# The output product of a fused attention and feed-forward kernel: from one product of 12 blocks to seven products of half blocks

## The chip, the cores and the metric

One core of one Trainium2 chip. The metric is device time in microseconds (us) of one execution of the whole program: the median of 3 runs is 566.71 us (566.59 to 567.5). Everything is computed on that core: TensorE (PE in the profile, with its weight loads PEld), VectorE (DVE), ScalarE (ACT), GpSimd (POOL) and SyncE (SP, here a queue that issues DMAs).

## The reference

A low-rank attention (keys and values are first projected from 1024 positions to 64) is followed by a gated feed-forward block. The output product, the last line, is what the change touches.

```python
# q, k, v: (8 batches, 8 heads, 1024, 64); E, F: (64, 1024)
k_proj = einsum('ks,bhsd->bhkd', E, k)
v_proj = einsum('ks,bhsd->bhkd', F, v)
attn   = softmax(q @ k_proj.T / sqrt(64))
x      = (attn @ v_proj), heads side by side     # 8192 x 512
g      = x @ w_gate                              # 512 -> 1536
h      = g * sigmoid(g) * (x @ w_val)            # 8192 x 1536
out    = h @ w_out                               # 1536 -> 512, float32
```

## The kernel before

**Chunks and steps.** The 8192 rows of `x` are worked through in 16 chunks `c` of 512 rows (two per batch `b`, c = 2b and 2b+1). A chunk has 12 steps `f`, one for each block of 128 of the 1536 inner columns. A step computes, transposed (128 inner columns on the partitions, 512 rows along the free side), the gate `f_g` and the value `f_v`: four matmuls of 128x128 by 512 columns each (`f_mm`, L440). ACT takes tanh of the gate's half (L452); DVE makes `s1 = (th + 1) * g` (L459) and `hT = s1 * v` in bf16 (L464). With the missing factor 0.5 that is `h`, and `hT[c]` is a tile of 128 x 12 x 512.

**The output product** of chunk c is spread over the steps of chunk c+1: `f_y(c, n)`, n = 0 to 11, one per step, four matmuls of 512 columns (L478). Three `f_y` make one block of 128 rows of the output: 12 matmuls accumulate over the 12 blocks of `hT`, ACT evicts them with scale 0.5 (L488), and SP sends 256 KB out (L490). The product of chunk 0 falls into steps 4 to 11 of chunk 1. The product of the last chunk is at the end, alone: 9 `f_y`, then `f_y_last`, whose last group is 12 matmuls of 192 columns.

**Attention runs ahead, in slots.** Each step t has two slots, 2t (between `f_g` and `f_v`) and 2t+1 (after `f_y`). `place(b)` (L508) puts the pieces of batch b into slots from s0 = 48(b-1) on, that is from the first step of chunk 2(b-1). For b = 3 and up: the projection `u_KV` in slot s0, `u_KT` in s0+3, eight score pieces `u_S` in slots s0+6, s0+9, ... s0+27, each followed one slot later by `u_R` (row sums and reciprocal on DVE, L346 and L348) and `u_N` (the normalising product on POOL, L361, 128x512), and eight `u_PV` (one matmul of 512 columns and an ACT copy). So the even chunk has six `u_N`, the last of them in the slot of step 11, and the odd chunk has two, after step 0 and in step 2. Batch 1 is placed by its own table: its score pieces lie in steps 5 to 10 of chunk 1, the transposing DMA `u_AD(1, 0)` (SP, L316) of the first four normalised pieces follows them, and `u_PV(1, 0, 0)` needs its result in step 10 of chunk 1.

**Loads are issued by POOL.** The K, V and two Q loads of batch b lie in four slots from 48(b-1)-24 on (for b = 3 from -20): in steps 0, 1, 2 and 3 of an odd chunk, and ahead of everything else of their slot. The loads of batches 4 to 7 are in chunks 5, 7, 9 and 11. At the start, POOL issues the loads of the weights, `wo` (the output weights, `load_wo`, L125) last, in two halves of six blocks.

**Buffers.** PSUM has eight banks: two for the gate, two for the value, one for the output product, three (`"a"`) for attention. `hT` has two buffers, `ysb` (the evicted output) three, K and V two each.

Every engine takes its instructions in the order in which the program issues them, so a line of Python that comes earlier is ahead in each engine's queue:

```python
for t in range(NIT):                       # L689
    c, f = divmod(t, NFT)
    f_g(c, f, i)
    run_slot(2 * t)
    f_v(c, f, i)
    for a in ypart.pop(t, ()):             # the f_y of chunk c-1
        f_y(*a)
    run_slot(2 * t + 1)
```

Of the kernel before, what the change touches and what calls it, by code (L numbers as in the profile page):

```python
# [28 lines left out]
CW = 512  # L29
NIT = B * CH * NFT  # L30
BY_DMA = [(b, ch) for b in range(1, B) for ch in range(CH)]


@with_exitstack
def kernel(
# [23 lines left out]
    w_pool = ctx.enter_context(tc.tile_pool(name="weights", bufs=1))  # L59
    kv_pool = ctx.enter_context(tc.tile_pool(name="kv", bufs=2))  # L60
    q_pool = ctx.enter_context(tc.tile_pool(name="qbf", bufs=4))
    aw = ctx.enter_context(tc.tile_pool(name="aw", bufs=2))
    x_pool = ctx.enter_context(tc.tile_pool(name="xT", bufs=2))
    h_pool = ctx.enter_context(tc.tile_pool(name="hT", bufs=2))
    fw = ctx.enter_context(tc.tile_pool(name="fw", bufs=3))
    y_pool = ctx.enter_context(tc.tile_pool(name="ysb", bufs=3))
    ps_g = ctx.enter_context(tc.tile_pool(name="psg", bufs=2, space=bass.MemoryType.PSUM))
    ps_v = ctx.enter_context(tc.tile_pool(name="psv", bufs=2, space=bass.MemoryType.PSUM))
    ps_y = ctx.enter_context(tc.tile_pool(name="psy", bufs=1, space=bass.MemoryType.PSUM))
    ps_a = ctx.enter_context(tc.tile_pool(name="psa", bufs=3, space=bass.MemoryType.PSUM))  # L70

# [10 lines left out]
    wv = w_pool.tile([P, NKT, DFF], BF16, name="wv")  # L82
    wo = w_pool.tile([P, NFT, DM], BF16, name="wo")

    kb, vb, qb, xT, hT = {}, {}, {}, {}, {}
# [45 lines left out]
    kvp = {}  # L131
    banks = {"a": (ps_a, "pa"), "g": (ps_g, "gps"), "v": (ps_v, "vps"), "y": (ps_y, "yps")}

    def bank(where, shape, dt, name):
        pool, tag = banks[where]
        return pool.tile(shape, dt, name=name, tag=tag)
# [152 lines left out]
    qT, ee, rr, AA, AT = {}, {}, {}, {}, {}  # L289

    def u_T(b, u, at="a", eng=nc.scalar):
        ch, w = divmod(u, 4)
        g, i = divmod(w, 2)
        ps = bank(at, [P, 4, P], BF16, "qTp")
        src = qb[b, ch]
        for n in range(4):
            nc.tensor.transpose(  # L297
                out=ps[:, n, :],
                in_=src[:, 4 * g + n, 2 * i : 2 * i + 2, :].rearrange("p j d -> p (j d)"),
                identity=ident_bf[:],  # L300
            )
        t = aw.tile([P, 4, P], BF16, name="qT", tag="qT", bufs=4)
        copy(eng, t[:], ps[:])
        qT[b, u] = t
# [46 lines left out]
    def u_N(b, u, eng=nc.gpsimd):  # L351
        ch, w = divmod(u, 4)
        g, i = divmod(w, 2)
        if (b, ch) in BY_DMA:
            if (b, ch, "d") not in AA:
                AA[b, ch, "d"] = aw.tile([P, 4, H, KP], BF16, name="AAd", tag="AAd")
            a = AA[b, ch, "d"][:, 2 * i : 2 * i + 2, 4 * g : 4 * g + 4, :]
        else:
            a = AA[b, u] = aw.tile([P, 2, 4, KP], BF16, name="AA", tag="AA", bufs=4)
            a = a[:]  # L360
        eng.tensor_tensor(  # L361
            out=a.rearrange("p j h k -> p h j k"),
            in0=ee.pop((b, u))[:],
            in1=rr.pop((b, u))[:].unsqueeze(3).to_broadcast([P, 4, 2, KP]),
            op=ALU.mult,
        )

    def u_A(b, u, eng=nc.vector):
        ch, w = divmod(u, 4)
        g, i = divmod(w, 2)  # L370
        if (b, ch) not in AT:
            AT[b, ch] = aw.tile([P, 4, NPAIR, P], BF16, name="AT", tag="AT")
        ps = ps_a.tile([P, 2, 2, P], BF16, name="aTp", tag="pa")
        a = AA.pop((b, u))
# [9 lines left out]
    def u_PV(b, ch, pr, eng=nc.scalar):  # L384
        if (b, ch) not in xT:
            xT[b, ch] = x_pool.tile([P, NPAIR, CW], BF16, name="xT", tag=f"xT{ch}")
        ps = ps_a.tile([P, CW], FP32, name="pv", tag="pa")
        nc.tensor.matmul(  # L388
            out=ps[:].rearrange("p (j t) -> p j t", t=P),
            lhsT=BDV[b % 2][:, pr, :],  # L390
            rhs=AT[b, ch][:, :, pr, :],
            start=True,
            stop=True,
        )
        copy(eng, xT[b, ch][:, pr, :], ps[:])

    def u_PV2(b, ch, g, i, eng):

        if (b, ch) not in xT:
            xT[b, ch] = x_pool.tile([P, NPAIR, CW], BF16, name="xT", tag=f"xT{ch}")  # L400
        ps = ps_a.tile([P, 2, CW // 2], FP32, name="pv", tag="pa")
        for n in range(2):
# [9 lines left out]
    def u_PV1(b, ch, pr, i, eng):  # L412

        ps = ps_a.tile([P, CW // 2], FP32, name="pv", tag="pa")
        nc.tensor.matmul(
# [39 lines left out]
    def f_v(c, f, i=None):  # L455
# [6 lines left out]
        if f == 0:  # L462
            hT[c] = h_pool.tile([P, NFT, CW], BF16, name="hT", tag="hT")
        nc.vector.tensor_tensor(out=hT[c][:, f, :], in0=s1[:], in1=ps[:], op=ALU.mult)  # L464

    yy = {}

    def f_y(c, n):
        i, part = divmod(n, 3)
        if part == 0:  # L470
            yy[c] = bank("gvgv"[i] if c == B * CH - 1 else "y", [P, DM], FP32, "yps")
        y_mm(c, i, range(4 * part, 4 * part + 4), slice(0, DM))
        if part == 2:
            y_out(c, i, slice(0, DM), nc.sync)

    def y_mm(c, i, fs, cs):
        for f in fs:
            nc.tensor.matmul(  # L478
                out=yy[c][:, cs],
                lhsT=hT[c][:, f, i * P : (i + 1) * P],  # L480
                rhs=wo[:, f, cs],
                start=(f == 0),
                stop=(f == NFT - 1),
            )

    def y_out(c, i, cs, eng):
        ysb = y_pool.tile([P, DM], FP32, name="ysb", tag="ysb")
        nc.scalar.activation(out=ysb[:, cs], in_=yy[c][:, cs], func=AF.Copy, scale=0.5)  # L488
        b, ch = divmod(c, CH)
        eng.dma_start(  # L490
            out=out[b * S : (b + 1) * S, :].rearrange("(p j) c -> p j c", j=NJ)[:, 4 * ch + i, cs],
            in_=ysb[:, cs],
        )

    def f_y_last(c, i):

        for cs, where in ((slice(0, 320), "v"), (slice(320, DM), "g")):
            yy[c] = bank(where, [P, DM], FP32, "yps")
            y_mm(c, i, range(NFT), cs)
            y_out(c, i, cs, nc.scalar)  # L500

# [39 lines left out]
    with tc.manual_schedule():  # L541
# [3 lines left out]
        for i in range(2):  # L545
# [3 lines left out]
            )  # L549
        ef = [const.tile([KP, S], dt, name=f"{n}raw") for n, dt in (("E", FP32), ("F", BF16))]  # L550
        nc.sync.dma_start(out=ef[0][:], in_=E)
# [130 lines left out]

        ypart = defaultdict(list)
        for c in range(B * CH - 1):
            for n in range(NFT):
                f = n if c else 4 + (2 * n + 1) // 3
                ypart[(c + 1) * NFT + f].append((c, n))

        for t in range(NIT):  # L689
            c, f = divmod(t, NFT)  # L690
            i = 1 if t < 2 else None
            f_g(c, f, i)
            run_slot(2 * t)
            f_v(c, f, i)
            for a in ypart.pop(t, ()):
                f_y(*a)
            run_slot(2 * t + 1)
        for n in range(9):
            f_y(B * CH - 1, n)
        f_y_last(B * CH - 1, 3)  # L700
        assert not slots and not ypart

# [28 lines left out]
```

## Time and profile before

| | |
|---|---|
| median of 3 runs | 566.71 us (566.59, 566.71, 567.5) |
| span of the profiled execution | 564.7 us |
| PE busy | 555.2 us, 98% of the span, 2917 matmuls in the trace |
| DVE, ACT, POOL busy | 339.5 (60%), 235.5 (42%), 111.9 us (20%) |
| matmuls of the output product (L478), 512 columns | 741 in the trace, 189.8 us |
| DVE `s1` and `hT` (128x512) | 679 and 688 ns each, 192 of each |
| ACT eviction of the output (128x512) | 597 ns each |
| POOL `u_N` (128x512) | 1041 ns each |
| last matmul group to the end of the span | eviction from 561.77 us, end at 564.7 |

The execution that was profiled has no run time of its own beside its span; the runs' median lies 2.0 us above the span, which is taken as a constant outside it. Times below are in us from the span's start. In the tables of the trace a line reads: start, duration, engine, source line, operation, output <- inputs, shape, count, and in brackets the idle time of that engine just before and what ended it. The duration of one matmul runs to the end of its result (379 ns for 512 columns) and overlaps the next one; the pace is read from the distance of starts. A few per cent of the matmuls are missing from the trace.

### The profile page before, as it was taken

The page shows a single profiled execution, that of the slowest core. Times are in us where ns is not written, and L with a number is a line of the kernel's source. Part 1 is how long each engine was busy: PE and PEld are TensorE (multiplying, and loading weights), DVE is VectorE, ACT ScalarE, POOL GpSimd, SP SyncE. Part 2 cuts the span into 40 slices and gives each one's busy share as a digit, 9 for nine tenths or more (in the row PEclk, how much of TensorE's full clock was granted, in tenths as well). Part 3 has the DMA queues.
Part 4 walks back from the last instruction along what each step waited for, and adds up shares of the span by engine and source line. Part 5 has one row for each costly group of instructions (what it writes and reads, how often), then busy time and mean ns, then how long its engine had stood idle before and what let it go on. Part 6 is the DMA issues. An engine that isn't in the chain of part 4 may idle for free.

```text
span 564.7 us, 7892 instructions
## 1 busy us (share of the span) xinstructions
PE 555.2 (98%) x2917; PEld 266.0 (47%) x2972; DVE 339.5 (60%) x579; ACT 235.5 (42%) x417; POOL 111.9 (20%) x126
## 2 busy tenths in 40 slices
PE   8999999999999999999999999999999999999997
PEld 4654544444444444444444444444444444444444
DVE  3787764766476655666556755667547665545550
ACT  3564352443444333543435434354243543443222
POOL 6851250133012400133002230024100220000000
PEclk9999999999999999999999999999999999999999
DMA  9999999529903894129920499106990212100012
GB/s 203 191 199 189 179 156 203 110 59 206 202 21 73 133 209 88 38 57 182 193 56 36 80 190 197 39 19 114 194 177 19 64 39 67 38 37 37 21 39 93
DMA packets 112215, 62.78 MB, mean 111 GB/s; under 512 B 66352, under 2 KB 103472, under 8 KB 112176
## 3 DMA queue, kind: packets, MB, share of 16 engines
q0 software_dynamic: 43952, 29.49, 36.5%
q1 hardware_dynamic: 67392, 31.46, 26.0%
q10 hardware_dynamic: 832, 1.31, 0.8%
q8 instruction: 23, 0.38, 0.3%
q14 instruction: 16, 0.13, 0.1%
HBM read 60.29 MB, written 16.78 MB: 136 GB/s over the span
## 4 chain that ended last, share of the span: by engine, by line
PE 95%; DMA 2%; POOL 1%; issue 1%; ACT 0%; POOLq 0%
PE vps L440 29%; PE yps L478 29%; PE gps L440 29%; PE sc L331 2%; PE pv L388 2%; DMA wv<-in_moe_w_val_dram 2%; PE kvp L151 2%; POOL vb L100 0%; POOL qb L109 0%; PE kvp L175 0%; PE kvp L190 0%; PE qTp L297 0%; PE kTp L252 0%; PE yps L440 0%; POOL kb L90 0%
## 5 line engine op out<-in xcount | busy, mean ns | idle before, releaser
L459 DVE SCALAR_TENSOR_TENSOR s<-th,gps 128x512 f32<-128x512 f32 x191 | 129.7, 679 | 132.7 <-ACT th L452 132.3
L440 PE MATMUL vps<-xT,wv 128*128 128x512 bf16 (+1 forms) x759 | 195.8, 377 | 1.9 <-DMA wv<-in_moe_w_val_dram 0.8
L440 PE MATMUL gps<-xT,wg 128*128 128x512 bf16 (+1 forms) x750 | 193.7, 377 | 0.8
L478 PE MATMUL yps<-wo,hT 128*128 128x512 bf16 (+2 forms) x765 | 192.6, 376 | 0.7
L452 ACT ACTIVATE th<-gps 128x512 f32<-128x512 f32 x191 | 114.0, 597 | 159.8 <-PE gps L440 139.9
L464 DVE TENSOR_TENSOR hT<-s,vps 128x512 bf16<-128x512 f32 x192 | 132.0, 688 | 20.8 <-DVE s L459 0.5
L361 POOL TENSOR_TENSOR AAd<-ee,rr 128x512 bf16<-128x512 f32 x56 | 58.2, 1041 | 340.9 <-issue 221.7
L478 PEld LDWEIGHTS <-hT 128*128 128x128 bf16 x780 | 76.2, 98 | 89.9
L440 PEld LDWEIGHTS <-wv 128*128 128x128 bf16 x776 | 73.9, 98 | 84.2 <-issue 3.0
L440 PEld LDWEIGHTS <-wg 128*128 128x128 bf16 x776 | 74.0, 98 | 80.9 <-issue 0.6
L488 ACT ACTIVATE ysb<-yps 128x512 f32<-128x512 f32 (+1 forms) x65 | 38.4, 590 | 77.7 <-PE yps L478 72.4
L139 ACT CAST xT<-pv 128x512 bf16<-128x512 f32 (+1 forms) x63 | 36.2, 578 | 52.3 <-PE pv L388 50.3
L346 DVE TENSOR_REDUCE zz<-ee 128x8 f32<-128x512 f32 x64 | 43.5, 679 | 22.0 <-ACT ee L335 21.9
L335 ACT ACTIVATE ee<-sc 128x512 f32<-128x512 f32 x64 | 37.9, 596 | 18.3 <-PE sc L331 17.1
L331 PEld LDWEIGHTS <-qTd 128*128 128x128 bf16 x224 | 17.1, 98 | 13.4 <-DMA qTd<-qb 0.7
L388 PE MATMUL pv<-AT,BDV 128*128 128x512 bf16 x60 | 22.4, 379 | 0.1
L331 PE MATMUL sc<-BD,qTd 128*128 128x128 bf16 x224 | 21.7, 219 | 0.1
L348 DVE RECIPROCAL rr<-zz 128x8 f32<-128x8 f32 x64 | 13.0, 203 | 6.3
L109 POOL DMA_DIRECT2D qb<-in_q_dram x18 | 16.3, 910 | 0.8 <-POOLq L715 0.8
L151 PE MATMUL kvp<-kb,ET 128*64 128x512 bf16 (+1 forms) x64 | 13.6, 355 | 0.0
L163 DVE CAST BDV<-kvp 64x256 bf16<-64x256 f32 x6 | 2.6, 426 | 17.8 <-ACT ks L159 17.8
L151 PE MATMUL kvp<-vb,FT 128*64 128x512 bf16 x48 | 11.5, 382 | 0.0
(82 smaller groups left out, 141.2 us busy)
## 6 DMA issues: line engine op xcount, KB each, us to landing
out_dram<-ysb SPq DMA_DIRECT2D x63, 256.0 KB, 2.3
qb<-in_q_dram POOLq DMA_DIRECT2D x14, 512.0 KB, 17.8
kb<-in_k_dram POOLq DMA_DIRECT2D x7, 1024.0 KB, 11.3
vb<-in_v_dram POOLq DMA_DIRECT2D x7, 1024.0 KB, 14.2
wo<-in_moe_w_out_dram POOLq DMA_DIRECT2D x2, 768.0 KB, 21.4
kraw<-in_k_dram ACTq DMA_DIRECT2D x2, 512.0 KB, 4.8
qb<-in_q_dram POOLq DMA_DIRECT2D x4, 256.0 KB, 7.9
wg<-in_moe_w_gate_dram POOLq DMA_DIRECT2D x4, 256.0 KB, 7.7
```

Of the source, the lines that this page charges most:

```text
L139: (nc.scalar.copy if eng is nc.scalar else eng.tensor_copy)(out=out, in_=in_)
L151: nc.tensor.matmul(out=t[lo : lo + 64, h0:h1].rearrange("p h d -> p (h d)"), lhsT=w[:, j, :], rhs=src[b][:, h0:h1, j, :], start=(j == 0), ...
L331: nc.tensor.matmul(out=ps[:, n, :], lhsT=t[:, n, :], rhs=BD[b % 2][:, 4 * g + n, :], start=True, stop=True)
L335: nc.scalar.activation(out=e[:].rearrange("p h j k -> p (h j k)"), in_=ps[:].rearrange("p a k -> p (a k)"), func=AF.Exp, scale=scale,)
L346: nc.vector.reduce_sum(out=z[:], in_=e[:], axis=AX.X)
L361: eng.tensor_tensor(out=a.rearrange("p j h k -> p h j k"), in0=ee.pop((b, u))[:], in1=rr.pop((b, u))[:].unsqueeze(3).to_broadcast([P, 4, 2 ...
L440: nc.tensor.matmul(out=ps[:, ts], lhsT=(wg, wv)[w][:, kt, f * P : (f + 1) * P], rhs=x[:, kt, ts], start=(kt == 0), stop=(kt == NKT - 1),)
L452: nc.scalar.activation(out=th[:], in_=ps[:], func=AF.Tanh, scale=0.5)
L459: nc.vector.scalar_tensor_tensor(out=s1[:], in0=th[:], scalar=1.0, in1=g[:], op0=ALU.add, op1=ALU.mult)
L464: nc.vector.tensor_tensor(out=hT[c][:, f, :], in0=s1[:], in1=ps[:], op=ALU.mult)
L478: nc.tensor.matmul(out=yy[c][:, cs], lhsT=hT[c][:, f, i * P : (i + 1) * P], rhs=wo[:, f, cs], start=(f == 0), stop=(f == NFT - 1),)
L488: nc.scalar.activation(out=ysb[:, cs], in_=yy[c][:, cs], func=AF.Copy, scale=0.5)
```

## The change

The output product of chunks 1 to 15 is computed as a two by two block product in Strassen's way. `hT[c]` is cut into quarters by inner half (blocks 0 to 5, 6 to 11) and row half (256 rows each), `wo` by inner half and column half (256 columns). Seven products of half blocks take the place of eight: for each block p of 128 rows in a row half there are seven groups `m_mm` of 6 matmuls with 256 columns, 84 matmuls of 256 columns in a chunk where there were 48 of 512.

- `w_sum(m)`: five sums or differences of quarters of `wo` (128 x 6 x 256, bf16), once, on DVE, in steps 2 to 6 of chunk 1.
- `h_sum(c, m)`: five sums or differences of quarters of `hT[c]` (128 x 6 x 256, bf16) per chunk, on POOL. Those for products 5 and 2 are made in six pieces of 256 elements in steps 6 to 11 of the chunk itself, those for 1, 6 and 7 whole, in steps 0, 1 and 2 of the next. In the last chunk 1 and 7 are made on DVE in pieces.
- `f_m(c, n)`, n = 0 to 13, in steps 12n//14 of chunk c+1, makes the products in the order 3, 4, 5, 2, 1, 6, 7 for p = 0 (steps 0, 0, 1, 2, 3, 4, 5) and again for p = 1 (steps 6, 6, 7, 8, 9, 10, 11).
- The results are combined by ACT (`m_X`, one copy of 512), DVE (`m_Y` 512, `m_W` 256, `m_Z` 512 columns) and POOL (256 in `m_X`, 512 in `m_Z`), and SP sends 512 KB per p.
- The output product has two PSUM banks, `yp0` ("y") and `yp1` ("z"); attention keeps two. Until the end of chunk 1 a third bank of attention is the second of these.
- `hT` takes the factor 0.5 (a `scalar_tensor_tensor` in the place of a `tensor_tensor`). K, V, and `xT` get one buffer each, `ysb` two buffers of 1024 floats; the tiles of batch 0's attention and of E and F share memory with the new tiles.
- `f_m_last` takes the place of the last chunk's `f_y` and `f_y_last`.

The diff, cut to its core (the tail of some calls is shortened):

```diff
+NC = B * CH
+HF = NFT // 2
+HC = DM // 2
+HT = CW // 2
...
-    kv_pool = ctx.enter_context(tc.tile_pool(name="kv", bufs=2))
+    kv_pool = ctx.enter_context(tc.tile_pool(name="kv", bufs=1))
...
-    ps_a = ctx.enter_context(tc.tile_pool(name="psa", bufs=3, space=bass.MemoryType.PSUM))
+    ps_a = ctx.enter_context(tc.tile_pool(name="psa", bufs=2, space=bass.MemoryType.PSUM))
...
+    ring = {"n": 0, "wide": True}
     def bank(where, shape, dt, name):
+        if where == "a" and ring["wide"]:
+            where = "aaz"[ring["n"] % 3]
+            ring["n"] += 1
...
-        nc.vector.tensor_tensor(out=hT[c][:, f, :], in0=s1[:], in1=ps[:], op=ALU.mult)
+        nc.vector.scalar_tensor_tensor(
+            out=hT[c][:, f, :], in0=s1[:], scalar=0.5, in1=ps[:], op0=ALU.mult, op1=ALU.mult
+        )
...
+    def quarter(t, half, x):
+        return t[:, HF * half : HF * (half + 1), HC * x : HC * (x + 1)]
+    def w_sum(m):
+        (a, b), op = {
+            1: (((0, 0), (1, 1)), ALU.add),
+            3: (((0, 1), (1, 1)), ALU.subtract),
+            4: (((1, 0), (0, 0)), ALU.subtract),
+            6: (((0, 0), (0, 1)), ALU.add),
+            7: (((1, 0), (1, 1)), ALU.add),
+        }[m]
+        nc.vector.tensor_tensor(out=ws[m][:], in0=quarter(wo, *a), in1=quarter(wo, *b), op=op)
+    def h_sum(c, m, f0, f1, eng=nc.gpsimd):
...
+        fs = slice(f0, f1)
+        eng.tensor_tensor(
+            out=hs[c, m][:, fs, :],
+            in0=quarter(hT[c], *a)[:, fs],
+            in1=quarter(hT[c], *b)[:, fs],
+            op=op,
+        )
+    def m_mm(c, p, m, ps):
+        for f in range(HF):
+            if m == 3:
+                lhsT = hT[c][:, f, p * P : (p + 1) * P]
+            elif m == 4:
+                lhsT = hT[c][:, HF + f, HT + p * P : HT + (p + 1) * P]
+            else:
+                lhsT = hs[c, m][:, f, p * P : (p + 1) * P]
+            rhs = {2: wo[:, f, 0:HC], 5: wo[:, HF + f, HC:DM]}.get(m)
+            nc.tensor.matmul(out=ps, lhsT=lhsT, rhs=ws[m][:, f, :] if rhs is None else rhs,
+                             start=(f == 0), stop=(f == HF - 1))
+    def m_X(c, p):
+        xs = d_pool.tile([P, 2, HC], FP32, name="xs", tag="d")
+        nc.scalar.copy(out=xs[:], in_=ym.pop((c, p, "X"))[:])
+        t = d_pool.tile([P, HC], FP32, name="tt", tag="t", bufs=2)
+        nc.gpsimd.tensor_tensor(out=t[:], in0=xs[:, 0], in1=xs[:, 1], op=ALU.add)
...
+    def m_Y(c, p):
+        nc.vector.tensor_tensor(out=ysb[:, 1:3], in0=xs[:], in1=Y[:], op=ALU.add)
+    def m_W(c, p):
+        nc.vector.tensor_tensor(out=t[:], in0=t[:], in1=W[:, 0], op=ALU.add)
+    def m_Z(c, p, eng=nc.gpsimd):
+        nc.vector.tensor_tensor(out=d[:], in0=Z[:], in1=ysb[:, 1:3], op=ALU.subtract)
+        eng.tensor_tensor(out=ysb[:, 0::3], in0=d[:], in1=t[:].unsqueeze(1).to_broadcast([P, 2, HC]), op=ALU.add)
+        nc.sync.dma_start(out=rows_of(c)[:, p::2, :], in_=ysb)
+    def f_m(c, n):
+        p, n = divmod(n, 7)
+        m = (3, 4, 5, 2, 1, 6, 7)[n]
+        which, at, half = (
+            ("X", "y", 0), ("X", "y", 1), ("Y", "z", 0), ("Y", "z", 1), ("W", "y", 0), ("Z", "z", 1), ("Z", "z", 0),
+        )[n]
...
+        m_mm(c, p, m, ym[c, p, which][:, half])
+        if n in (1, 3, 4, 6):
+            {1: m_X, 3: m_Y, 4: m_W, 6: m_Z}[n](c, p)
+    def f_m_last(c):
...
+        m_mm(c, 0, 1, W[0][:, 0])
+        m_W(c, 0)
+        m_mm(c, 0, 7, Z[0][:, 0])
+        m_mm(c, 1, 1, W[1][:, 0])
+        m_Z(c, 0, nc.vector)
+        m_W(c, 1)
+        nc.vector.tensor_tensor(out=d[:], in0=t_broadcast, in1=ysb[:, 1:3], op=ALU.subtract)
+        for x in (1, 0):
+            if x == 0:
+                m_mm(c, 1, 7, Z[1][:, 0])
+            nc.vector.tensor_tensor(out=ysb[:, 3 * x], in0=d[:, x], in1=Z[1][:, x], op=ALU.add)
+            nc.scalar.dma_start(out=rows_of(c)[:, 1 + 2 * x, :], in_=ysb[:, 2 * x : 2 * x + 2])
...
+        late = defaultdict(list)
+        for n in range(NFT):
+            late[NFT + 4 + (2 * n + 1) // 3].append((f_y, 0, n))
+        for m, f in ((3, 2), (4, 3), (6, 4), (7, 5), (1, 6)):
+            late[NFT + f].append((w_sum, m))
+        for c in range(1, NC):
+            for f in range(HF):
+                for m in (5, 2):
+                    late[c * NFT + HF + f].append((h_sum, c, m, f, f + 1))
+                if c == NC - 1:
+                    for m in (1, 7):
+                        late[c * NFT + HF + f].append((h_sum, c, m, f, f + 1, nc.vector))
+            if c == NC - 1:
+                late[c * NFT + HF - 1].append((h_sum, c, 6, 0, HF))
+            else:
+                for i, m in enumerate((1, 6, 7)):
+                    late[(c + 1) * NFT + i].append((h_sum, c, m, 0, HF))
+                for n in range(14):
+                    late[(c + 1) * NFT + 12 * n // 14].append((f_m, c, n))
         for t in range(NIT):
...
+            ring["wide"] = c < 2
             f_g(c, f, i)
             run_slot(2 * t)
             f_v(c, f, i)
+            for fn, *a in late.pop(t, ()):
+                fn(*a)
             run_slot(2 * t + 1)
+        f_m_last(NC - 1)
```

## The prediction

> **What bounds the kernel now.** I read the page's first part, the chain that ended last, PE's waits, and then the timeline at the places that the change touches.
>
> ```profile
> PE 555.2 (98%) x2917; PEld 266.0 (47%) x2972; DVE 339.5 (60%) x579; ACT 235.5 (42%) x417; POOL 111.9 (20%) x126
> ...
> PE 95%; DMA 2%; POOL 1%; issue 1%; ACT 0%; POOLq 0%
> ```
>
> PE is busy throughout and is 95% of the chain; its largest wait in the whole span is 1.2 us. So the time is PE's, and each us taken from PE is a us gained as long as PE never waits. That is the question here, because the other engines now get work that PE must wait for. The granted clock is full in every slice.
>
> **What PE saves.** The pace is read from starts of groups of four matmuls: first with 256 columns (step 1 and its neighbours at the beginning), then with 512.
>
> ```profile
> 21.73 0.60 PE L440 MATMUL gps<-xT,wg 128*128 128x256 bf16 x4
> 22.17 0.60 PE L440 MATMUL vps<-xT,wv 128*128 128x256 bf16 x4
> 22.60 0.60 PE L440 MATMUL gps<-xT,wg 128*128 128x256 bf16 x4
> ...
> 266.80 1.03 PE L440 MATMUL vps<-xT,wv 128*128 128x512 bf16 x4
> 267.67 1.03 PE L478 MATMUL yps<-wo,hT 128*128 128x512 bf16 x4
> 268.53 1.03 PE L440 MATMUL gps<-xT,wg 128*128 128x512 bf16 x4
> ```
>
> Four of 256 columns, each with its own weight load, take 0.436 us (109 ns each); four of 512 take 0.865 us (216 ns). The halves cost half. A chunk's output product goes from 12 x 0.865 = 10.37 us to 84 x 0.109 = 9.17 us: 1.20 us in each of 15 chunks, **18.0 us off PE**. A step becomes 0.865 + 0.865 + 0.655 = 2.38 us (3.04 in steps 0 and 6).
>
> **What costs nothing.** `hT` as scalar_tensor_tensor: the row of `s1`, the same form, has 679 ns against 688. ACT loses four evictions of 0.6 us per chunk and gains two. DVE gains 2 x (0.69 + 0.42 + 0.69) = 3.6 us per chunk; over its densest stretch (even chunk, steps 3 to 11, 23.4 us of PE) it then has 12.4 (`s1`, `hT`) + 5.3 (six `u_R` of 0.89) + 2.5 = 20.2 us; two banks each for gate and value let it lag by one step. Without that cover each excess us would be PE's. Product banks: each is written again at least two steps (4.8 us) after its last product, and its evictions take 0.6 to 0.7 us. Two banks for attention: `u_S` comes every 1.5 steps, `u_PV` every step, an eviction ends 1 us after its matmul, so a bank is free over 3 us before its next use. One K and V buffer: batch b is loaded a chunk after batch b-1 was projected. One `xT` per half: written two steps or more after its last reader. SP: two DMAs of 512 KB for four of 256.
>
> **The end.** After the last chunk 14 groups take 9.17 us, counted above. Before, the last eviction began when the last matmul was out and took 0.33 us. Now DVE has, after product 7 of p = 0, a subtraction (0.69), an addition (0.69), `m_W` (0.42), a subtraction (0.69) and two additions of 256 (0.42 each): 3.3 us, of which 1.3 lie beside PE's last two groups. So the last row block is ready 2.0 us after PE instead of 0.35, and its DMA carries 256 KB (2.3 us to landing) where 96 KB took 1.7. **+2.25 us**, bounds 1 and 3.
>
> **Chunk 1: DVE waits for `wo`.** The rows are the second half of `wo` being issued, DVE in steps 2 and 3, PE's gate of step 5, and two places of batch 1:
>
> ```profile
> 33.58 0.83 POOL L125 DMA_DIRECT2D wo<-in_moe_w_out_dram  x1 [1.13 <-DMA qb<-in_q_dram]
> ```
>
> ```profile
> 51.55 0.69 DVE L464 TENSOR_TENSOR hT<-s,vps 128x512 bf16<-128x512 f32 x1
> 53.58 0.69 DVE L459 SCALAR_TENSOR_TENSOR s<-th,gps 128x512 f32<-128x512 f32 x1 [1.35 <-ACT th L452]
> ```
>
> ```profile
> 56.32 1.03 PE L440 MATMUL gps<-xT,wg 128*128 128x512 bf16 x4
> ...
> 75.61 0.38 PE L388 MATMUL pv<-AT,BDV 128*128 128x512 bf16 x1
> ```
>
> ```profile
> 69.00 3.34 SPq L316 DMA_TRANSPOSE AT<-AAd  x1
> ```
>
> That half of `wo` takes 23.4 us and lands at 57.0. `w_sum(3)` stands in DVE's queue right after `hT` of step 2 (ends at 52.2) and reads both halves, so DVE stands until 57.0, and `s1` of step 3 behind it, whose gate bank PE wants again at 56.32. No row is a bf16 sum in SBUF; DVE's bf16 copies have 426 ns for 512 (1536: 1.28 us), its one product of two float32 SBUF inputs 681 (2.04 us); below, half the copy (0.64). I take 1.28, the row of the same type. Then `s1(3)` ends at 57.0 + 1.28 + 0.7 = 59.0 (PE waits 2.7 us); after it `hT(3)` 0.7, the next sum 1.28, four BD casts 1.75 and `s1(4)` 0.7 end at 63.4, where PE arrives at 62.7 (0.7). The rest of DVE's queue (three sums, four `u_R`, `s1` and `hT`) brings the fourth `u_R` to 75.8, its `u_N` to 76.9; the transposing DMA, which took 6.1 us, then lands at 83.0 instead of 75.1. `u_PV` started at 75.61, now 79.0 with the delay so far: 4.0 us more. **+7.4 us**, bounds 2.1 (0.64 and no third wait) and 11 (2.04).
>
> **The odd chunks: POOL's queue.** This decides the forecast. POOL's pace, a V load, `u_N` and a Q load back to back:
>
> ```profile
> 74.55 0.88 POOL L100 DMA_DIRECT2D vb<-in_v_dram  x1
> 75.44 1.06 POOL L361 TENSOR_TENSOR AAd<-ee,rr 128x512 bf16<-128x512 f32 x1
> 76.43 0.94 POOL L109 DMA_DIRECT2D qb<-in_q_dram  x1
> ```
>
> A product of 512 occupies POOL 0.99 us, a load 0.9 to 0.96. The sums need a price for 1536 bf16 elements, x, and 256, h. No row has bf16 inputs. Above: `u_N` as recorded, 1041 ns for 512, gives x = 3.12; its pace gives 2.9 (h = 0.5). Below: a bf16 memset (204 ns for 128; one of a single element takes 0.10) gives 1.3. The same memset in float32 has 231 ns, so bf16 took a fifth less past the fixed part; I take `u_N`'s pace less a fifth, **x = 2.3, h = 0.4**.
>
> Let 0 be the end of the last value product of an even chunk (in chunk 6: 251.68).
>
> ```profile
> 251.68 0.81 PE L478 MATMUL yps<-wo,hT 128*128 128x512 bf16 x3
> ...
> 252.49 0.69 DVE L464 TENSOR_TENSOR hT<-s,vps 128x512 bf16<-128x512 f32 x1
> ```
>
> The last `hT` is ready at 1.5, DVE's `m_Z` at 2.2, POOL's part of it at 3.2. From there POOL has, in queue order: two h, K load 0.94, sum 1 (x), the sum of `m_X` 0.5, `u_N` 0.99, V load 0.9, sum 6 (x), Q load 0.94, `u_N` 0.99, sum 7 (x). So sum 7 is ready at 8.5 + 3x + 2h. PE wants it after the left-over group (0.66), five steps (one of 3.04, four of 2.38), two `u_S` of 0.22 and step 5's gate and value (1.73): 15.4. With x = 2.3 it comes at 16.2: PE waits 0.8 us in each of chunks 5, 7, 9, 11. Chunk 3 has its loads later (sum 7 ready at 14.4 against 15.8), chunks 13 and 15 have none: no wait. Even chunks have no loads, no `u_N` ahead and 1.85 us of `u_KV` on PE: 13.7 at x = 2.9 against 17. **+3.2 us.**
>
> The Trainium skill (GPSIMD Engine Reference, Elementwise — side-by-side cycle accounting) puts a two-input elementwise instruction of GpSimd at about 2.6 cycles per element at 1.2 GHz, which speaks against this change: 3.3 us for 1536, an estimate, and with it waits of some 21 us and a time near 580. `u_N`'s pace here (0.99 us for 512) is below that rule (1.11).
>
> **Sum**, against the profiled execution (span 564.7; the runs' median 566.7 is 2.0 more, kept): 566.7 - 18.0 + 2.25 + 7.4 + 3.2 = **561.5 us**.
>
> **Rivals.**
> *POOL is fast enough.* With x below 2.05 no chunk waits: 558.4, and 553 if chunk 1 costs only 2.1. For: memset's rows; against: `u_N` is the only row of the same operation.
> *Slower: sums at `u_N`'s pace.* One mechanism, product 7 of chunks 5 to 11 waiting for POOL: x = 2.9 gives 18.2 against 15.4, 2.8 us x 4, and 0.4 in chunk 3: 570. At x = 3.12 (3.5 x 4, 1.4 in chunk 3, 0.7 in 13 and 15) 575. It decides from x = 2.7, where four waits of 2.3 use up the 8.4 us that are left of the gain. For: the same opcode. Against: float32 inputs there.
> *The saving is not there.* If groups of 256 lost 14 ns per matmul (84 x 15 of them), 18 us are gone: 579. Against: the starts 0.436 us apart above, weight loads included.
>
> **Numbers.** Forecast 0.40 (its own range 558.5 to 565), fast POOL 0.27, sums at `u_N`'s pace 0.25, no saving or other waits 0.08. The range 553 to 572 leaves out the slowest sums and most of the last case. A difference of 0.2% (1.1 us) is about what a measurement of this kernel can tell from none. Faster: the first two and a little of the third, 0.68; within it 0.06; slower 0.26.
>
> **What would show it.** Groups of six matmuls 0.655 us apart; the POOL rows of 128x1536, which set x at once; PE waiting for POOL before product 7 in chunks 5, 7, 9, 11 and nowhere else; DVE idle until 57.0 in chunk 1, PE late at step 5 and at the first `u_PV`; 5 us from the last matmul to the end. The forecast is wrong if x is off by 0.3 (4 us), if `wo` lands earlier, or if DVE falls behind in the even chunks.

## The result and the profile after

The changed kernel takes **583.27 us** (median of 4 runs, 582.75 to 584.4) where the kernel before takes 566.85 (566.59 to 567.5): the ratio is 1.0289, with a 95% interval of 1.0274 to 1.0304. It is 2.9% slower, and the forecast of 561.5 (range 553 to 572) was wrong on the sign as well as the size. The profiled execution, with a span of 582.6 us, is the slowest of the four (584.4 us at a granted clock of 0.984; the others 582.75 to 583.67 at 0.987 or 0.988), so the account of it below lies about 1 us above the median. Line numbers of the changed kernel are about 20 to 90 higher than those of the kernel before: `f_g` and `f_v` are L462, `m_mm` L564, `h_sum` L547, `w_sum` L526, `u_N` L383, `u_PV` L410.

From the first page of the profile after, the engines, the granted clock in 40 slices and the chain that ended last:

```profile
PE 549.1 (94%) x3500; PEld 319.5 (55%) x3500; DVE 399.3 (69%) x689; ACT 217.9 (37%) x386; POOL 415.1 (71%) x407
...
PEclk9999999999999989999899999999999999999997
...
PE 61%; POOL 18%; DVE 8%; DMA 7%; issue 4%; ACT 1%; DVEq 0%; POOLq 0%
```

PE was 95% of the chain and is now 61%; POOL, which had 1%, has 18%. POOL's busy time went from 111.9 to 415.1 us. The clock, full before in every slice, drops in three. PE's busy time fell by 6.1 us only, though its work fell by 18.0; one reason is that some of its matmuls ran at half the clock.

What PE waited for, largest first (total us, times, longest us). `hs` are the sums of `hT`, `ysb` and `dd` are written where DVE combines the products, `s` is `s1`, and `AT` the transposed attention weights:

```profile
PE yps L564 <- POOL hs L547: 17.1, 10, 2.4
PE yps L564 <- DVE ysb L658: 2.4, 1, 2.4
PE yps L564 <- DVE dd L603: 2.2, 1, 2.2
PE gps L462 <- DVE s L481: 2.2, 2, 2.0
PE pv L410 <- DMA AT<-AAd: 1.2, 1, 1.2
```

The first row is the odd chunks, the second and third the end, the last two chunk 1. The groups by shape give the price that the forecast had bounded from both sides (busy us, mean ns of one, idle before):

```profile
L547 POOL TENSOR_TENSOR hs<-hT 128x1536 bf16<-128x1536 bf16 x43 | 132.9, 3097 | 0.2
L547 POOL TENSOR_TENSOR hs<-hT 128x256 bf16<-128x256 bf16 x180 | 117.5, 674 | 42.0 <-DVE hT L486 41.9
```

So x = 3.10 us for 1536 elements and h = 0.67 for 256: a fixed 0.19 us and 1.89 ns for each element ((3097 - 674) / 1280). The forecast had x = 2.3 and h = 0.4.

How these durations become waits is seen in chunk 5 (the 0 of the forecast's count lies at 186.16), in the timeline of all engines:

```profile
197.40 3.11 POOL L547 TENSOR_TENSOR hs<-hT 128x1536 bf16<-128x1536 bf16 x1
...
200.56 0.83 PE L564 MATMUL yps<-ws,hs 128*128 128x256 bf16 x6 [1.22 <-POOL hs L547]
...
202.37 3.09 POOL L547 TENSOR_TENSOR hs<-hT 128x1536 bf16<-128x1536 bf16 x1
...
205.52 1.46 PE L564 MATMUL yps<-ws,hs 128*128 128x256 bf16 x6 [2.40 <-POOL hs L547]
206.77 1.91 PE L462 MATMUL gps<-xT,wg 128*128 128x512 bf16 x4
...
208.48 1.15 PE L462 MATMUL vps<-xT,wv 128*128 128x512 bf16 x4
```

POOL has no gap: sum 6 (197.40), a Q load (200.43), a `u_N` (201.37), sum 7 (202.37). Sum 7 is ready at 205.46, which is 19.3 after the 0. Product 6 waits 1.22 us and product 7 another 2.40. After the second wait the next four matmuls of 512 columns start 1.71 us before the following group (206.77 to 208.48), where the kernel before took 0.865: PE runs at half its clock (granted 0.5 from 205.3 to 208.7). So a wait costs more than the row that shows it.

Where the time went, by the starts of the K and V projections of the even chunks, which lie two chunks apart: before, two chunks took 67.74 us. Chunks 4 and 5 now take 70.89, 6 and 7 71.05, 8 and 9 71.03, 10 and 11 69.34. With 2.4 us saved these four pairs lose 5.6, 5.7, 5.7 and 4.0. With 1.6 in chunk 3 and 1.5 together in chunks 13 and 15 that is 24.1 us. The whole account: 564.7 - 18.0 + 24.1 (odd chunks) + 3.9 (chunk 1) + 8.05 (end) = 582.8, against a span of 582.6.

### The profile page after: what moved, and what is told of

It is laid out like the page before. It is cut to its first block, busy times and chain, and to the rows that moved or that the text cites. A ratio compares the mean times of both kernels' runs of the same rounds, so it can differ in the third digit from the quotient of the medians.

```text
span 582.6 us, 9314 instructions
## 1 busy us (share of the span) xinstructions
PE 549.1 (94%) x3500; PEld 319.5 (55%) x3500; DVE 399.3 (69%) x689; ACT 217.9 (37%) x386; POOL 415.1 (71%) x407
## 4 chain that ended last, share of the span: by engine, by line
PE 61%; POOL 18%; DVE 8%; DMA 7%; issue 4%; ACT 1%; DVEq 0%; POOLq 0%
PE gps L462 19%; PE yps L564 18%; PE vps L462 18%; POOL hs L547 10%; DMA wo<-in_moe_w_out_dram 4%; POOL AAd L383 3%; DVE s L481 2%; PE pv L410 2%; PE kvp L162 2%; DVE hT L486 2%; DMA qb<-in_q_dram 1%; DMA Fraw<-in_F_dram 1%; DVE zz L368 1%; PE sc L353 1%; POOL qb L116 1%
## 5 line engine op out<-in xcount | busy, mean ns | idle before, releaser
L547 POOL TENSOR_TENSOR hs<-hT 128x256 bf16<-128x256 bf16 (+1 forms) x223 | 250.0, 1141 | 42.2 <-DVE hT L486 41.9
L462 PE MATMUL gps<-xT,wg 128*128 128x512 bf16 (+1 forms) x772 | 198.6, 380 | 2.2 <-DVE s L481 2.2
L462 PE MATMUL vps<-xT,wv 128*128 128x512 bf16 (+1 forms) x776 | 199.3, 380 | 0.9 <-DMA wv<-in_moe_w_val_dram 0.9
L486 DVE SCALAR_TENSOR_TENSOR hT<-s,vps 128x512 bf16<-128x512 f32 x192 | 132.1, 688 | 21.2 <-PE vps L462 1.2
L564 PEld LDWEIGHTS <-hs 128*128 128x128 bf16 x900 | 87.8, 99 | 62.9 <-POOL hs L547 22.0
L462 PEld LDWEIGHTS <-wv 128*128 128x128 bf16 x776 | 74.5, 99 | 85.9 <-issue 5.9
L462 PEld LDWEIGHTS <-wg 128*128 128x128 bf16 x776 | 74.5, 98 | 59.3 <-issue 4.2
L564 PE MATMUL yps<-ws,hs 128*128 128x256 bf16 x540 | 74.7, 276 | 19.4 <-POOL hs L547 17.1
L383 POOL TENSOR_TENSOR AAd<-ee,rr 128x512 bf16<-128x512 f32 x56 | 58.4, 1044 | 37.6 <-DVE rr L370 32.3
L604 POOL TENSOR_TENSOR ysb<-dd,tt 128x512 f32<-128x512 f32 x28 | 35.6, 1270 | 40.9 <-DVE dd L603 40.9
L564 PE MATMUL yps<-wo,hs 128*128 128x256 bf16 x360 | 48.9, 274 | 0.0
L564 PE MATMUL yps<-ws,hT 128*128 128x256 bf16 x360 | 46.2, 280 | 2.2 <-DVE dd L603 2.2
L564 PEld LDWEIGHTS <-hT 128*128 128x128 bf16 x360 | 36.2, 100 | 13.9 <-issue 3.4
L584 POOL TENSOR_TENSOR tt<-xs 128x256 f32<-128x256 f32 x30 | 21.8, 727 | 24.0 <-ACT xs L581 24.0
L603 DVE TENSOR_TENSOR dd<-yps,ysb 128x512 f32<-128x512 f32 x29 | 19.9, 686 | 10.6 <-PE yps L564 10.6
L410 PE MATMUL pv<-AT,BDV 128*128 128x512 bf16 x60 | 22.4, 379 | 1.3 <-DMA AT<-AAd 1.2
```

Of the source, the lines that this page charges most:

```text
L383: eng.tensor_tensor(out=a.rearrange("p j h k -> p h j k"), in0=ee.pop((b, u))[:], in1=rr.pop((b, u))[:].unsqueeze(3).to_broadcast([P, 4, 2 ...
L410: nc.tensor.matmul(out=ps[:].rearrange("p (j t) -> p j t", t=P), lhsT=BDV[b % 2][:, pr, :], rhs=AT[b, ch][:, :, pr, :], start=True, stop=True,
L462: nc.tensor.matmul(out=ps[:, ts], lhsT=(wg, wv)[w][:, kt, f * P : (f + 1) * P], rhs=x[:, kt, ts], start=(kt == 0), stop=(kt == NKT - 1),)
L486: nc.vector.scalar_tensor_tensor(out=hT[c][:, f, :], in0=s1[:], scalar=0.5, in1=ps[:], op0=ALU.mult, op1=ALU.mult)
L547: eng.tensor_tensor(out=hs[c, m][:, fs, :], in0=quarter(hT[c], *a)[:, fs], in1=quarter(hT[c], *b)[:, fs], op=op,)
L564: nc.tensor.matmul(out=ps, lhsT=lhsT, rhs=ws[m][:, f, :] if rhs is None else rhs, start=(f == 0), stop=(f == HF - 1),)
```

## The experiments

The theory: (1) POOL's sums cost x = 3.1, its queue delivers sums 6 and 7 too late in the odd chunks, and PE's clock halves after some of these waits; (2) the end and chunk 1 add the rest; (3) the saving on PE is all there. The rivals: the products of half blocks don't save what the starts promised; the fewer buffers and PSUM banks cost something; the loss is the sums themselves, wherever they stand, and not their place in POOL's queue. Times are medians; each ratio is against the kernel before on the same chip, with its 95% interval.

### No sums at all

```diff
-                lhsT = hs[c, m][:, f, p * P : (p + 1) * P]
+                h = HF if m == 7 else 0
+                lhsT = hT[c][:, h + f, p * P : (p + 1) * P]
...
-            for f in range(HF):
-                for m in (5, 2):
-                    late[c * NFT + HF + f].append((h_sum, c, m, f, f + 1))
...
```

> The changed kernel without the sums of hT: products 1, 2, 5, 6 and 7 read a quarter of hT in the place of a sum, so the output is not the reference's. Theory (the 24 us lost in the odd chunks are PE waiting for POOL's sums, and the clock that drops after such a wait): 583.3 - 24 - about 5 for the wait of the first u_PV and DVE's pieces in the last chunk, so 552 to 557. Rival (the products of 256 columns, their banks or their evictions cost PE the time): 575 or more, since all of these stay.

Measured: **556.14 us**, ratio 0.9813 (0.9793 to 0.9832). Two chunks take 65.36 us in every pair from chunk 4 on: 67.74 - 65.36 = 2.38, so 1.19 per chunk against 1.20 forecast. The saving on PE is there to the last tenth; what the change lost, it lost in the sums and the waits. The largest of PE's waits that stay:

```profile
PE yps L565 <- DVE ysb L659: 2.4, 1, 2.4
```

The wait of 2.4 at the end is there without any sum, so it isn't made by them (see the end below).

### Only the buffers and banks of the change, in the kernel before

```diff
-    kv_pool = ctx.enter_context(tc.tile_pool(name="kv", bufs=2))
+    kv_pool = ctx.enter_context(tc.tile_pool(name="kv", bufs=1))
...
-    ps_a = ctx.enter_context(tc.tile_pool(name="psa", bufs=3, space=bass.MemoryType.PSUM))
+    ps_a = ctx.enter_context(tc.tile_pool(name="psa", bufs=2, space=bass.MemoryType.PSUM))
...
```

(`xT` and `ysb` likewise.)

> The kernel before with only the buffers of the change: two PSUM banks for attention from chunk 2 on, one K, one V and one xT buffer per half, two ysb. Theory (an eviction ends long before its bank is wanted again): 566.3 to 567.3, no change. Rival (part of the loss is attention waiting for its banks or loads for their buffers): 568.5 or more.

Measured: 566.69 us, ratio 0.999 (0.998 to 1.0). Two banks for attention and single buffers for K, V and `xT` cost nothing, as the forecast had it. This rival is out.

### The loads out of the odd chunks

```diff
-            s0 = 48 * (b - 1) - (20 if b == 3 else 24)
+            s0 = 60 if b == 3 else 48 * (b - 2) + 8
```

> The changed kernel with the loads of batches 3 to 7 moved from the odd chunk to the even chunk before it (steps 4 to 7, behind the sums). Theory (POOL's queue in order): three loads of 0.93 us leave the way of sum 7, which comes at 16.5 instead of 19.3 after the end of the chunk, where PE wants it at 15.4: a wait of 1.1 us in chunks 5, 7, 9 and 11 instead of 4.0, too short for the clock to drop: about 566 to 569. Rival (the loads do not matter, POOL is late anyway): 580 or more.

Measured: **569.08 us**, ratio 1.0045 (1.0029 to 1.006): 14.2 us less than the change. The same sums, on the same engine, in the same steps; only the four loads now lie in the even chunk, three of which (2.8 us of POOL's time) had been ahead of sum 7. PE's wait for `hs` shrinks from 17.1 to 5.0 us, its longest from 2.4 to 1.0. So the place in POOL's queue decides, not the sums as such.

### The loads and the last two `u_N` behind sum 7

```diff
+            late_n = b > 2 and j > 5
-            put(sa[j] + 1, u_N, b, j)
+            put(s0 + 29 if late_n else sa[j] + 1, u_N, b, j)
```

(with the edit of the kernel above, and `u_R` likewise.)

> As e2_loads, and the two u_N that lie ahead of sum 7 in the odd chunks (batches 3 to 7) moved behind it. Theory (POOL's queue in order): two times 1.05 us less ahead of sum 7, ready at 14.4 against 15.4 us after the chunk: no wait for POOL in any chunk, 5 to 6 us less than e2_loads, 562 to 565. Rival (what is left in e2_loads has another cause): 568 or more.

Measured: **561.76 us**, ratio 0.9916 (0.9902 to 0.9929). Another 7.3 us less, a little under the 562 expected; of the waits of the odd chunks none is left, and two chunks take 65.36 us, as without any sum. This closes the account of the odd chunks: 583.27 - 561.76 = 21.5 us came back by order alone. The other 2.6 of their 24.1 are lost again ahead of chunk 4, where the loads of batch 3 now lie: batch 3's projection starts at 154.57 (153.61 in the change) although chunk 3's 1.6 are gone, and two waits, 2.1 us together, for the transposed Q (`qTd`) are new. What is still missing to 556.14, 5.6 us, lies there and at the end: from the projection of batch 2 to that of batch 3 it takes 57.63 us where the kernel without sums takes 55.18, and from the last group of chunk 14's product to the end of the span 18.7 against 15.9. Chunk 1 is no part of it: `w_sum` stands there in both.

### Sum 7 of the odd chunks on DVE

```diff
+                    eng = nc.vector if m == 7 and (c + 1) % 2 else nc.gpsimd
-                    late[(c + 1) * NFT + i].append((h_sum, c, m, 0, HF))
+                    late[(c + 1) * NFT + i].append((h_sum, c, m, 0, HF, eng))
```

> The changed kernel with sum 7 of the odd chunks on DVE instead of POOL. Theory: DVE makes 1536 bf16 in 0.95 us (its sums of wo), so the wait before product 7 goes and the 1.4 us before product 6 stay: 563 to 568. Rival (DVE's sum with two SBUF inputs and a POOL sum hold each other up, as in the last chunk where two DVE pieces took 3.46 us during a POOL sum): DVE falls behind by 2 to 3 us per chunk, 573 or more.

Measured: 576.56 us, ratio 1.0168 (1.0154 to 1.0182). The first theory (DVE does it in about 1 us) fell, the rival held. DVE's sum of the same size in `w_sum`, four of the five with POOL idle, took 0.95 us; here it has, in the groups by shape of this kernel, 4.6:

```profile
L547 DVE TENSOR_TENSOR hs<-hT 128x1536 bf16<-128x1536 bf16 x7 | 32.3, 4615 | 0.0
```

Chunk 5 of this kernel shows what lies beside it:

```profile
195.21 1.06 POOL L383 TENSOR_TENSOR AAd<-ee,rr 128x512 bf16<-128x512 f32 x1
...
195.59 5.48 DVE L547 TENSOR_TENSOR hs<-hT 128x1536 bf16<-128x1536 bf16 x1
...
197.15 3.10 POOL L547 TENSOR_TENSOR hs<-hT 128x1536 bf16<-128x1536 bf16 x1
```

DVE's sum begins while POOL works on a `u_N` (195.21 to 196.27), and ends (201.07) 0.8 us after POOL's V load (issued at 196.19) and its whole sum (to 200.25) are over. POOL's sum isn't slowed (3.10), DVE's is. The other way round POOL loses: in the changed kernel the last sum of `wo` began just ahead of two POOL pieces (68.59 and 68.75) and kept its 0.95 us, and the two pieces took 1.94 us instead of 1.29. Behind it in DVE's queue stands `m_Y`, and PE now waits for that: 11.7 us in all. The Trainium skill (SBUF — State Buffer, SBUF: two separate sides) says that a DVE instruction with two SBUF inputs and a GpSimd instruction that reads SBUF exclude each other for the whole instruction. These rows agree, but for one thing that this run adds: DVE's sum, first in line, did not run between POOL's product and POOL's sum either, 0.9 us in which POOL issued a load, and so stood through all three, 5.48 us where 0.95 were needed.

### The last chunk as before

The last chunk's product in the old form, alone at the end, with no sums for it:

```diff
-        f_m_last(NC - 1)
+        for n in range(9):
+            f_y(NC - 1, n)
+        f_y_last(NC - 1, 3)
...
```

(The lines that leave out its sums and give `f_y` its banks at the end are not shown.)

> The changed kernel with the last chunk's output product made as before (48 products of 512 columns, no sums in the last chunk). Theory (the end lost 6.9 us: DVE's pieces in the last chunk, the bank of the last product held by an addition, the clock after both waits): 575.5 to 577.5. Rival (the last chunk is not dearer than forecast, PE gives back the 1.2 us saved there): 582 or more.

Measured: 577.84 us, ratio 1.0188 (1.0171 to 1.0205): 5.4 us less than the change, although 1.2 us of PE's saving go with it, and 0.3 us above the range of the theory; PE's wait for POOL stays at 17.1. In the changed kernel the end looked so (DVE, POOL, then PE, out of the timeline):

```profile
549.90 3.09 POOL L547 TENSOR_TENSOR hs<-hT 128x1536 bf16<-128x1536 bf16 x1
...
550.41 3.46 DVE L547 TENSOR_TENSOR hs<-hT 128x256 bf16<-128x256 bf16 x2
...
566.62 3.55 PE L564 MATMUL yps<-ws,hT 128*128 128x256 bf16 x18 [2.23 <-DVE dd L603]
...
577.36 1.44 PE L564 MATMUL yps<-ws,hs 128*128 128x256 bf16 x6 [2.36 <-DVE ysb L658]
```

DVE's pieces for the last chunk (two of 256 take 3.46 us beside POOL's sum) make DVE late, so `m_Z` of the chunk before frees its bank 2.2 us late. And the very last product (7 of p = 1) writes one half of a bank whose other half DVE must read first: it waits 2.4 us for that addition, at half clock after it. This second wait is the one that stood in the kernel without sums.

### Chunk 1: `w_sum` later, one sum first that needs only the first half of `wo`

```diff
-        for m, f in ((3, 2), (4, 3), (6, 4), (7, 5), (1, 6)):
+        for m, f in ((6, 2), (3, 4), (4, 5), (7, 6), (1, 7)):
...
-                    late[c * NFT + HF + f].append((h_sum, c, m, f, f + 1))
+                    late[c * NFT + (HF + f if c > 1 else max(9, HF + f))].append((h_sum, c, m, f, f + 1))
```

> The changed kernel with the sums of wo in another order (6 in step 2, which needs only the first half of wo; 3, 4, 7 and 1 in steps 4 to 7) and chunk 1's pieces of sums 5 and 2 not before step 9. Theory (DVE stood 4.6 us for wo, then u_N behind the pieces made the first u_PV late): the 3.9 us of chunk 1 go, 579 to 580.5. Rival (DVE has no room for the sums in chunk 1 in any order): 582.5 or more.

Measured: 581.62 us, ratio 1.0265 (1.0249 to 1.0281): 1.65 us less, between the two cases. In the changed kernel chunk 1 reads (DVE first, then PE):

```profile
56.91 0.96 DVE L526 TENSOR_TENSOR ws<-wo 128x1536 bf16<-128x1536 bf16 x1 [4.63 <-DMA wo<-in_moe_w_out_dram]
```

```profile
58.52 1.02 PE L462 MATMUL gps<-xT,wg 128*128 128x512 bf16 x4 [2.00 <-DVE s L481]
...
79.56 0.39 PE L410 MATMUL pv<-AT,BDV 128*128 128x512 bf16 x1 [1.23 <-DMA AT<-AAd]
```

At the next gate PE waits 0.2 more. With the edit these waits are gone, but a new one of 1.6 us stands in their place: PE now arrives earlier at batch 2's projection, and its V load isn't there until 94.9. In the changed kernel it landed at 95.9, 0.9 us before PE wanted it: chunk 1's lateness had hidden it.

### All three together

The edits of the last two kernels and of the one with the `u_N` moved, in one.

> e5_nlate, e6_tail and e7_chunk1 together: no wait for POOL in the odd chunks, the old end, chunk 1 without its two waits. Theory (the losses are separate and add): 583.3 - 24 + 4 (waits too short for POOL, 0 to 4) - 6.8 - 3.4, so 549 to 554, below both kernels. Rival (the waits cover one another and come back elsewhere): 558 or more.

Measured: **555.59 us**, ratio 0.9811 (0.979 to 0.9833): 1.9% faster than the kernel before and 4.7% faster than the change. The three gains add up nearly: 583.27 - 21.5 - 5.4 - 1.65 = 554.7. That is 1.6 us above the range expected (549 to 554), whose terms for the end and chunk 1 were larger than what those two edits had each brought, and below the rival's 558. Its execution that was profiled took 558.84 us, the four others 555.25 to 555.88. The granted clock differs too, 0.994 against 0.999 to 1.0: in the profiled one the pace is half for 3.4 us twice, from 7.2 us, at the start, and from 126.7, behind a wait of 2.1 us for `qTd`. How much of the 3.3 us that makes isn't shown, and the waits of this execution are the upper side:

```profile
PE sc L353 <- DMA qTd<-qb: 3.6, 3, 2.1
PE kvp L162 <- DMA vb<-in_v_dram: 1.4, 1, 1.4
```

None is for POOL's sums but one of 0.2. Fourteen chunks save 16.8 us on PE, and 11.1 arrive; the rest is chunk 1 (the first `u_PV` starts 2.0 us later than before) and transfers that were hidden behind the slower product; it is not divided further here.

### Batch 2's loads two to four slots earlier

```diff
-            at = (43, 43, 44, 45) if b == 2 else (s0, s0 + 2, s0 + 4, s0 + 6)
+            at = (40, 41, 40, 42) if b == 2 else (s0, s0 + 2, s0 + 4, s0 + 6)
```

(on top of all three.)

> e8_all with the loads of batch 2 moved from slots 43 to 45 to slots 40 to 42, ahead of the pieces of sums 5 and 2 in POOL's queue. Theory (in e8_all PE waits 1.4 us for batch 2's V and 2.4 us for its Q, which POOL issues behind ten pieces, and the clock drops after them): 3 to 5 us less than e8_all, 550.5 to 553. Rival (HBM is the bound there, the loads land no earlier): 555 or more.

Measured: 564.66 us, ratio 0.9955 (0.9943 to 0.9967): 9 us slower than the version above instead of faster. The theory fell. The wait for the V load is gone, and one of 8.4 us came in another place; POOL, SP and PE in the timeline:

```profile
70.85 0.94 POOL L97 DMA_DIRECT2D kb<-in_k_dram  x1
...
70.93 3.56 SPq L338 DMA_TRANSPOSE AT<-AAd  x1
...
84.39 0.61 PE L410 MATMUL pv<-AT,BDV 128*128 128x512 bf16 x1 [8.39 <-DMA AT<-AAd]
```

The K load now starts together with batch 1's transposing DMA. That DMA landed 13.4 us after its issue, where it took 4.8 in the version above (issued at 72.35, loads from 80.67 on). (Its next one there, issued at 88.74 beside the loads, took 15.3 us as well, but PE never waited for it.) So 3 MB of loads beside a transposing DMA nearly tripled its time, and the old slots, just behind it, had been the right ones. Whether the 16 DMA engines or the memory set the pace isn't told apart by this run.

### What a wait of PE costs

In the kernel before, 12 waits are made on purpose (steps 6 and 10 of chunks 3 to 13, the odd ones): POOL adds n elements of `hT` to themselves, and one small matmul needs the result.

```diff
+    def f_gap(c, f, n):
+        src = hT[c][:, f + 1 - n // CW : f + 1, :]
+        nc.gpsimd.tensor_tensor(
+            out=dummy[:, 0:n].rearrange("p (a t) -> p a t", t=CW), in0=src, in1=src, op=ALU.add
+        )
+        ps = bank("a", [P, P], FP32, "dps")
+        nc.tensor.matmul(out=ps[:], lhsT=dummy[:, n - P : n], rhs=ident_bf[:], start=True, stop=True)
...
+            if c % 2 and c > 1 and c < 15 and f in (6, 10):
+                f_gap(c, f, 512)
```

n = 512:

> The kernel before with a wait of PE put in at 12 places (steps 6 and 10 of the odd chunks 3 to 13): POOL adds the hT of the step to itself (512 elements) and one matmul of 128 columns uses it. Nothing of the output changes. The waits are about 1.3 us each. If a wait costs its length: 566.7 + 12 x 1.36, 583. If PE's clock drops after it, as after the longer waits of the changed kernel, up to 1.7 us more each: 590 or more. Theory: too short for that, 581 to 585.

n = 1024:

> As g1_gap512 with 1024 elements, waits of about 2.3 us. If a wait costs its length: 566.7 + 12 x 2.36, 595. Theory (a wait of this length drops the clock in most places and then costs 1.6 us more): 603 to 616 and a mean clock below 0.98.

n = 1536:

> As g1_gap512 with 1536 elements, waits of about 3.2 us. If a wait costs its length: 566.7 + 12 x 3.26, 606. Theory (the clock drops after nearly each wait, 1.6 us more): 618 to 628 and a mean clock lower than in g2_gap1024.

| n | median us | ratio | mean granted clock (profiled run) | longer per wait | longest wait shown |
|---|---|---|---|---|---|
| 512 | 589.73 | 1.0392 (1.035 to 1.0434) | 0.999 | 1.93 | 1.9 |
| 1024 | 609.76 | 1.0742 (1.0696 to 1.0787) | 0.983 | 3.60 | 2.7 |
| 1536 | 630.38 | 1.1096 (1.1049 to 1.1143) | 0.962 | 5.31 | 3.6 |

The kernel before had 566.6 on that chip; "longer per wait" is the difference over 12. The mean waits shown are 1.68, 2.53 and 3.38 us, and the emptying of PE (0.17: a group of four lasts 1.03 us where the next could start after 0.865) and the small matmul (0.06) come on top: 1.90, 2.75 and 3.61. The remainder is 0, 0.85 and 1.7 us per wait, in the mean: in the timelines the pace is half behind none of the 12 waits for n = 512, behind six for 1024 (1.7 us each) and behind ten for 1536 (2.0 each). The expected 581 to 585 and 618 to 628 were exceeded by 4.7 and 2.4 us, because the waits came out longer than 1.3 and 3.2; 609.76 lies in its range, with a clock a little above the 0.98 expected. In the timeline of n = 1536:

```profile
139.72 0.29 PE L511 MATMUL dps<-ident_bf,dummy 128*128 128x128 bf16 x1 [3.56 <-POOL dummy L507]
139.80 1.91 PE L440 MATMUL gps<-xT,wg 128*128 128x512 bf16 x4
141.50 1.91 PE L440 MATMUL vps<-xT,wv 128*128 128x512 bf16 x4
```

Groups start 1.70 us apart where they take 0.865: half the clock, here for three groups (to 144.92). A wait of 1.7 us costs what is shown, one of 3.4 half as much again. The Trainium skill (TensorE: Matmul & The Clock Gate, Part 1, What's actually happening) says that the clock falls to half after an idle window of about 3.4 us, and that the windows run freely. The halving and the chance in it agree: the same 2.4 us of wait in chunk 11 were followed by full pace, in chunks 5, 7 and 9 not. Chunk 11 reads:

```profile
418.49 0.83 PE L564 MATMUL yps<-ws,hs 128*128 128x256 bf16 x6 [2.42 <-POOL hs L547]
419.16 1.03 PE L462 MATMUL gps<-xT,wg 128*128 128x512 bf16 x4
420.02 1.03 PE L462 MATMUL vps<-xT,wv 128*128 128x512 bf16 x4
```

But here an idle time shorter than 3.4 us was enough, down to 2.0 us: in chunk 1 of the kernel with the loads moved the group behind such a wait is followed by one at half the pace (59.49, the next at 61.18), where the same wait in the changed kernel (2.00, above) is not.

```profile
58.63 1.05 PE L462 MATMUL gps<-xT,wg 128*128 128x512 bf16 x4 [2.02 <-DVE s L481]
59.49 1.89 PE L462 MATMUL vps<-xT,wv 128*128 128x512 bf16 x4
```

## Why the prediction was wrong

**The step that failed is the price of the sums**: "The same memset in float32 has 231 ns, so bf16 took a fifth less past the fixed part; I take `u_N`'s pace less a fifth, x = 2.3, h = 0.4". It measured 3.10 and 0.67, and PE waited 17.1 us for the sums instead of 3.2. The row of the same operation (`u_N`, 1041 ns recorded for 512, which the prediction turned into 3.12) was right within 1% for x; the discount, taken from an instruction without inputs, was not. The rule of the Trainium skill (GPSIMD Engine Reference, Elementwise — side-by-side cycle accounting) that the prediction weighed against it, 2.6 cycles per element, by estimate 3.3 us for 1536 and a time near 580, was 7% too high in the duration and the nearest of all to the time. I set it aside because `u_N`'s pace (0.99) was below it (1.11); that is 11%, where the value taken was 30% below it. (Two slips in the working of the case of sums at `u_N`'s pace: 0.99 us for 512 are 2.97 for 1536, not 2.9, and at x = 2.7 the four waits come to 2.1, not 2.3. Neither changes the forecast.)

**The mechanism was right.** The count "8.5 + 3x + 2h" gives, with the measured values, 8.5 + 9.3 + 1.3 = 19.1; sum 7 was ready at 19.3. Wanted at 15.4, that is a wait of 3.7; 1.22 + 2.40 = 3.62 came, the first part already at product 6, where no wait had been expected, as in chunks 3 and 13. The terms of the rival with sums at `u_N`'s pace, for x = 3.12 (3.5 us in four chunks, 1.4 in chunk 3, 0.7 in 13 and 15) make 16.8; the trace has 17.1.

**What no case had: the clock.** The odd chunks lost 24.1 us, of which 17.1 are waits. After them the pace was half in three of four chunks; the inserted waits put that at 1.7 to 2.0 us each time, and the three pairs that show it lose 1.6 us more than the one with chunk 11: 4.8. The emptying of PE before each of ten waits (0.17) makes 1.7; together 23.6. So from this alone the rival's 575 was too low by 6.5 us.

**The end** was forecast at 2.25 (bounds 1 and 3) and took 20.35 us from the last group of chunk 14's product to the end of the span, against 13.5 before: 6.85 more, and 8.05 with the 1.2 saved. The working counted instructions behind the last matmul. It left out that DVE's pieces meet POOL's (2.2 us of wait), that product 7 shares a bank with the half that is read before it (2.4), and the half clock after both (1.4 for 18 matmuls, 0.6 for the last six). These make 6.6, where 5.8 are to be explained; from the last matmul (578.8) to the end it took 3.8 us instead of 5.

**Chunk 1** was forecast at 7.4 (bounds 2.1 and 11) and took 3.9. DVE did stand until 56.9 (57.0 forecast), and the waits at step 5, the next and `u_PV` are where they were put; `w_sum` took 0.95 instead of 1.28 us, and the queue behind it recovered faster: 2.0, 0.2 and 1.2 us instead of 2.7, 0.7 and 4.0.

**Right as forecast:** 1.20 us per chunk on PE (1.19 measured, in three kernels), groups of six 0.655 us apart, and nothing for banks and buffers (ratio 0.999).

By parts, forecast and measured: PE -18.0 and -18.0; odd chunks +3.2 and +24.1; chunk 1 +7.4 and +3.9; end +2.25 and +8.05. The first error alone turns a gain into a loss.

## What to carry to other kernels

Before a step is given to an engine that had been idle, add up that engine's whole queue between the inputs' arrival and the moment the result is wanted, at the price of the nearest row of the same operation without a discount, and order the queue by due time: here moving four loads and two products behind the sums was worth 21.5 us, more than the 18 that the change takes off PE. Count a wait of PE of about 2 us or more for more than its length, because the clock may halve behind it. And expect that each gain uncovers a transfer that was just in time.

## What the runs showed of the hardware

- A POOL sum of two bf16 inputs takes 0.19 us and 1.89 ns per element (674 ns for 256, 3097 for 1536); for 512 that gives 1.16 us, between the 1.04 of the product with float32 inputs (`u_N`) and the 1.27 of the float32 sum in `m_Z`; the float32 sum of 256 in `m_X` takes 0.73. So against a float32 sum the bf16 sums are 7 to 9% shorter, not a fifth (the access in `m_Z` differs as well), and against `u_N` they are not shorter at all.
- PE's clock can halve after waits of 2.0 us and more, for about 3.4 us (205.3 to 208.7 in chunk 5) or longer, not always: behind none of 12 waits of 1.7 us, six of 12 of 2.5 and ten of 12 of 3.4; mean extra cost 0, 0.85 and 1.7 us.
- A DVE sum of two SBUF inputs beside POOL's work took 4615 ns in the mean where 953 are needed alone; POOL's sums weren't slowed (3097). Where DVE's sum was first, POOL's two pieces took 1.94 us instead of 1.29.
- A transposing DMA of 4.8 us took 13.4 beside 3 MB of loads.
